# Wo read in 8 KB runs for pairs of heads, the two halves of each value product joined before the gather

## The chip, the cores and the metric

One core of a Trainium2 chip runs the kernel. The engines named here are PE (TensorE matmul, with its weight loads listed apart as PEld), DVE (VectorE), ACT (ScalarE), POOL (GpSimd) and SP (SyncE, which here only issues DMAs). The metric is the device time of one execution in microseconds. Before the change three runs gave 120.51, 120.59 and 120.69 us, with 120.59 us as their median.

## The reference, cut to what matters

```python
xn = layernorm(x)                              # x: 8 rows of 512
q  = (xn @ wq)                                 # 32 heads of 128
k, v = last 1024 positions of the caches       # 8 key-value heads, 4 query heads on each
p  = softmax(q k^T / sqrt(128))
s  = concat_heads(p v) @ wo                    # wo: 4096 x 512
h  = (gelu(xn @ w_gate) * (xn @ w_up)) @ w_down
out = x + s * silu(h)                          # 8 x 512
```

All tensors are bf16. The work is a decode step: the caches of eight sequences and the weights, 47 MB in all, are read once, and little is computed on each byte.

## The kernel before, in words

**Loads.** SP issues every large load in program order into nine rotating 2 MB buffers named big: wq, w_gate, w_up, then per key-value head one K tile and one V tile (2 MB each, in 8 KB runs per partition), w_down in between, and at the end wo. `load_wo` (L127) reads wo in five DMAs, listed in `pieces` (L623 to L625): four heads at once, two heads, one head, then three quarters and the last quarter of head 7. The 4096 rows of wo are laid out so that partition p of a head holds that head's rows 4p to 4p+3: a run of 4 KB.

**The loop.** A set s (16 of them, NS) is half of a key-value head's eight sequences: four sequences, 128 partitions. The loop at L571 runs half steps t, with s, i = divmod(t, 2). One half step writes to the engines' queues, in this order: the exponentials of set s-2 (ACT, L488), a transpose of a quarter of K (PE, L433) copied out by DVE (L444), on odd half steps from s = 6 the `gather` of a finished head (L580), another quarter of K copied out by ACT (L446), the transpose of the probabilities (DVE, L498), the scores of set s-1 (PE L455, then one DVE pass L463 that masks and takes the maximum), the maxima across partitions (PE L474, DVE L479), and half of a value product of the set (t - 9) / 2 (`value_half`, L504: eight PE matmuls, L509). The engines work through these queues in order; what an engine waits for holds back everything queued behind it.

**Values and gather.** The value product of a set lands in one PSUM bank, o_ps, as two halves of 128 columns, because V is read two positions to a partition row; only one half is meant for a given partition. ACT copies both halves to blk (L516, 128 x 256). A POOL copy (L492) puts the row sums beside the second half. `gather` (L520) multiplies, on PE, four times per head with a mask (sums) that picks the right half and adds up the partitions: 128 columns out, fp32. Then DVE takes the reciprocal of the row sum (L531), divides (L533), and turns the head's 128 x 128 block into oL (L541), which is the weight side of the output projection. The gather's result m_out and the maxima's result m_top lie in the same PSUM tile, m_ps.

**Projection.** After the loop, `project` (L609) runs four matmuls of 128 columns per query head (128 in all, L615) in the order of `pieces`, each piece waiting for its DMA; then two DVE operations (L633, L634) combine with g_sb and xf, and two small DMAs write the output.

Of the kernel before, what the change touches and what calls it, by code (L numbers as in the profile page):

```python
# [8 lines left out]
ACT = mybir.ActivationFunctionType  # L9
ALU = mybir.AluOpType  # L10
AX = mybir.AxisListType
BF16 = mybir.dt.bfloat16
FP32 = mybir.dt.float32
# [4 lines left out]
def kernel(  # L18
# [13 lines left out]
    nc = tc.nc  # L32

    B, Sq, D = A_x.shape
    Hkv, Sk, Dh = A_k_cache.shape[1], A_k_cache.shape[2], A_k_cache.shape[3]
    Hq = A_wq.shape[1] // Dh
    rep = Hq // Hkv
# [5 lines left out]
    scale = float(Dh) ** -0.5  # L43
    P = nc.NUM_PARTITIONS
# [6 lines left out]
    G = 4  # L51
    NB = B // G
# [4 lines left out]
    SET = NCH * Dh  # L57
# [3 lines left out]
    DP = Dh // 2  # L61
    NQB = D // 128
    PB = 32 // B

    NG = 2
    NS2 = NQB // NG
# [4 lines left out]
    big = ctx.enter_context(tc.tile_pool(name="big", bufs=9))  # L71
# [13 lines left out]


    m_ps = ps_m.tile([P, 512], FP32, name="m_ps")
    m_top, m_out = m_ps[:, 0:P], m_ps[:, P : P + Dh + 1]


    x_sb = rows.tile([B, D], BF16, name="x_sb")
# [23 lines left out]
                nc.sync.dma_start(out=t[:, y, :], in_=src[y])  # L115
        return [t[:, y, :].rearrange("p (c d) -> p c d", c=NCH) for y in range(NB)]

    HB = 2 * SET // (rep * D)
    wo_tiles = {}

    def wo_at(h):

        if h // HB not in wo_tiles:
            wo_tiles[h // HB] = big.tile([P, HB, rep * D], BF16, name="big")
        return wo_tiles[h // HB]

    def load_wo(h, r0, n, nh=1):  # L127

        t = wo_at(h)[:, h % HB : h % HB + nh, r0 * D : (r0 + n) * D]
        nc.sync.dma_start(  # L130
            out=t if nh > 1 else t[:, 0, :],
            in_=A_wo[h * rep * Dh : (h + nh) * rep * Dh, :].rearrange(
                "(h p r) n -> p h (r n)", p=P, r=rep
            )[:, :, r0 * D : (r0 + n) * D]
            if nh > 1
            else A_wo[h * rep * Dh : (h + 1) * rep * Dh, :].rearrange(
                "(p r) n -> p r n", r=rep
            )[:, r0 : r0 + n, :],
        )
        return [t[:, i, :].rearrange("p (r n) -> p r n", r=n) for i in range(nh)]  # L140

    wq_rows = []
    for k0, cuts in ((0, (1, 1)), (2, (2,))):
        t = big.tile([P, 2, Hq * Dh], BF16, name="big")
        i = 0
# [93 lines left out]
    quarter = consts.tile([P, NS2 + 32], FP32, name="quarter")  # L239
    nc.gpsimd.memset(quarter, 0.0)  # L240
    gsel = lead.tile([P, G], FP32, name="gsel")
    sums = consts.tile([P, 2, 2, rep, B, PB], FP32, name="sums")
    nc.gpsimd.memset(sums, 0.0)
    qT = qT0.rearrange("p (e s c g j) -> p e s c g j", e=2, c=2, g=G, j=rep)


    OW = 32
    OL = rep * OW
    oL = rows.tile([P, NS2 * (Hkv + 1), OL + 1], BF16, name="oL")
    nc.gpsimd.memset(oL, 0.0)  # L250

    def masks():
        nc.vector.tensor_reduce(
            out=parts, in_=identf.rearrange("p (x n) -> p n x", n=NC),
            axis=AX.X, op=ALU.max,
        )
        nc.vector.tensor_reduce(
            out=gsel, in_=parts.rearrange("p (g j) -> p g j", j=rep),
            axis=AX.X, op=ALU.max,
        )  # L260
        nc.vector.tensor_reduce(
            out=half, in_=identf.rearrange("p (r c n) -> p c r n", c=2, n=NC),
            axis=AX.XY, op=ALU.max,
        )
        nc.vector.tensor_reduce(
            out=quarter[:, NS2 : NS2 + B * NS2 : NS2],
            in_=identf.rearrange("p (a b f) -> p f b a", b=B, f=PB)[:, 0],
            axis=AX.X, op=ALU.max,
        )

        nc.vector.tensor_scalar(
            out=gsel, in0=gsel, scalar1=-1.0, scalar2=-NEG, op0=ALU.add, op1=ALU.mult
        )
        nc.vector.tensor_copy(
            out=own.rearrange("p c b g -> p (c b) g"),
            in_=gsel.unsqueeze(1).to_broadcast([P, CP * 32 // G, G]),
        )

        m = small.tile([P, NC], FP32, name="m16")
        nc.vector.tensor_scalar(  # L280
            out=m, in0=parts, scalar1=-1.0, scalar2=-NEG, op0=ALU.add, op1=ALU.mult
        )
        nc.vector.tensor_copy(
            out=same, in_=m.unsqueeze(1).to_broadcast([P, NR * 2, NC])
        )
        for c in range(2):
            for b in range(2):
                nc.vector.tensor_scalar(
                    out=sums[:, c, b].rearrange(
                        "p j (g y) f -> p y j g f", y=NB  # L290
                    )[:, b],
                    in0=parts.rearrange("p (g j) -> p j g", j=rep)
                    .unsqueeze(3).to_broadcast([P, rep, G, PB]),
                    scalar1=half[:, c : c + 1], scalar2=None, op0=ALU.mult,
                )

    hT = rows.tile([P, NFC, 32], BF16, name="hT")
# [7 lines left out]
    for k in range(NDC):  # L305
        w = wq_rows[k]
        for t in range(NT):
            for g in range(NQB):
# [3 lines left out]
                    w[:, 0, h * HD : (h + 1) * HD],  # L312
                    start=(k == 0), stop=(k == NDC - 1), skip_group_check=True,
                )
    q_row = rows.tile([P, NT, rep, 2, 2, DP], BF16, name="q_row")
    for c in range(2):
        nc.vector.tensor_copy(  # L317
            out=q_row[:, 0, :, :, c, :],
# [91 lines left out]

    def fold():

        f_sb = rows.tile([P, D], FP32, name="f_sb")
        nc.scalar.activation(out=f_sb, in_=f_state["ps"], func=ACT.Copy)
        spread(m_top, quarter, f_sb)
        f_state["ps"] = m_top[0 : 32 * NG]
# [66 lines left out]
        biases[s] = bias  # L483

    def exponentials(s):
        blk[s] = small.tile([P, 2, Dh + 1], FP32, name="blk", bufs=6)
        P_[s] = p_pool.tile([P, CP * 32], BF16, name="p")
        nc.scalar.activation(  # L488
            out=P_[s], in_=sc.pop(s), func=ACT.Exp, scale=scale, bias=biases.pop(s),
            accum_out=blk[s][:, 0, Dh : Dh + 1],  # L490
        )
        nc.gpsimd.tensor_copy(  # L492
            out=blk[s][:, 1, Dh : Dh + 1], in_=blk[s][:, 0, Dh : Dh + 1]
        )

    def turn(s):
# [2 lines left out]
            out=pT[s].rearrange("p c k -> p (c k)"), in_=P_.pop(s)  # L499
        )  # L500

    o_ps = {}

    def value_half(s, i):  # L504
        if i == 0:
            o_ps[s] = ps_o.tile([P, 2, Dh], FP32, name="o_ps")
        for c in range(i * CP // 2, (i + 1) * CP // 2):
            q = c % NR
            nc.tensor.matmul(  # L509
                o_ps[s][32 * q : 32 * q + 32].rearrange("p c d -> p (c d)"),  # L510
                pT[s][:, c, :],
                V[s][:, 2 * c : 2 * c + 2, :].rearrange("p c d -> p (c d)"),
                start=(c < NR), stop=(c >= CP - NR), skip_group_check=True,
            )
        if i == 1:
            nc.scalar.activation(out=blk[s][:, :, 0:Dh], in_=o_ps.pop(s), func=ACT.Copy)  # L516
            pT.pop(s)
            V.pop(s)

    def gather(h):  # L520

        ps = m_out
        for b in range(NB):
            t = blk.pop(h * NB + b)
            for c in range(2):
                nc.tensor.matmul(  # L526
                    ps, sums[:, c, b].rearrange("p j b f -> p (j b f)"), t[:, c, :],
                    start=(b == 0 and c == 0), stop=(b == NB - 1 and c == 1),
                )
        rec = small.tile([P, 1], FP32, name="rec")  # L530
        nc.vector.reciprocal(out=rec, in_=ps[:, Dh : Dh + 1])  # L531
        o = small.tile([P, rep, Dh // rep], BF16, name="o")
        nc.vector.tensor_scalar(  # L533
            out=o, in0=ps[:, 0:Dh].rearrange("p (i r) -> p r i", r=rep),
            scalar1=rec, scalar2=None, op0=ALU.mult,
        )


        out = oL[:, NS2 * h : NS2 * h + PB, 0:OL]
        out = out.rearrange("p f (r y) -> p r y f", y=OW)  # L540
        nc.vector.transpose(  # L541
            out=out[:, :, 0 : B * NS2 : NS2, :], in_=o.rearrange("p r i -> p (r i)")
        )


# [25 lines left out]
    for t in range(2 * NS + LV + 3):  # L571
# [3 lines left out]
        if s < NS:  # L575
            if i == 0 and s % NB == 0:
                fetch("K", s // NB)
            transpose_quarter(s, 2 * i)
        if i == 1 and s >= 6 and s % 2 == 0:
            gather((s - 6) // 2)  # L580
        if s < NS:
            transpose_quarter(s, 2 * i + 1)
        for _ in range(2):
# [5 lines left out]
            scores(s - 1)  # L589
        if i == 1 and 0 <= s - 1 < NS:  # L590
            maxima(s - 1)
        if t == LV - 1:
            fetch("D", 0)
            down(0)
# [11 lines left out]

    s_ps = ps_s.tile([32 * NG, 128], FP32, name="s")

    def project(h, r, w):  # L609
        t = oL[:, NS2 * h : NS2 * (h + 1)].rearrange("p f y -> p (f y)")  # L610
        for s in range(NS2):
            a = s * OL + r * OW
            for g in range(NG):
                q = NG * s + g
                nc.tensor.matmul(  # L615
                    s_ps[32 * g : 32 * g + 32, :], t[:, a : a + OW],
                    w[:, q * 128 : (q + 1) * 128],
                    start=(h == 0 and r == 0 and s == 0),
                    stop=(h == Hkv - 1 and r == rep - 1 and s == NS2 - 1),
                    skip_group_check=True,  # L620
                )

    pieces = [(0, 0, rep, 4), (4, 0, rep, 2), (6, 0, rep, 1)]  # L623

    pieces += [(Hkv - 1, 0, rep - 1, 1), (Hkv - 1, rep - 1, 1, 1)]  # L625
    for h0, r0, nr, nh in pieces:
        t = load_wo(h0, r0, nr, nh)
        for h in range(h0, h0 + nh):
            for r in range(r0, r0 + nr):
                project(h, r, t[h - h0][:, r - r0, :])  # L630
    tmp = small.tile([32 * NG, 128], FP32, name="tmp", bufs=1)
    out_sb = small.tile([32 * NG, 128], BF16, name="out_sb", bufs=1)
    nc.vector.tensor_tensor(out=tmp, in0=s_ps, in1=g_sb, op=ALU.mult)  # L633
# [36 lines left out]
```

## Time and profile before

| what | value |
|---|---|
| median of three runs | 120.59 us |
| time of the profiled execution | 120.65 us |
| span of the profiled execution | 118.8 us |
| bytes moved by DMA | 47.60 MB in 6569 packets |
| DMA queue q1 (SP's loads) | 95.2% of 16 engines over the span |
| PE / PEld busy | 84.4 us (71%) / 59.2 us (50%) |
| DVE / ACT / POOL busy | 66.3 (56%) / 56.2 (47%) / 7.5 us (6%) |

The span is the profiler's time from the first to the last instruction; the remaining 1.85 us of the execution lie around it. Busy times overlap between engines, so they do not add up to the span. An engine that is busy for 71% of the span may still have the last word in a stretch at the end, which is why stretches are looked at one by one.

### The profile page before, as it was taken

What the parts mean: (1) busy time and instruction counts of PE and PEld (TensorE: products, weight loads), DVE (VectorE), ACT (ScalarE), POOL (GpSimd) and SP (SyncE); (2) the same over time, 40 slices, a digit from 0 to 9 for tenths busy, and PEclk for the clock granted to TensorE, in tenths of its full rate; (3) what the DMA queues carried; (4) which work ended last, traced back from release to release, by engine and by line L of the source; (5) the groups of instructions that cost most, each with busy time, mean ns of one, the idle gap of its engine ahead of it and who ended that gap; (6) DMA issues with size and microseconds to landing.
All of it is one profiled execution on the core that took longest, in us unless ns stands there. A gap on an engine that the chain in (4) does not pass through costs nothing.

```text
span 118.8 us, 2387 instructions
## 1 busy us (share of the span) xinstructions
PE 84.4 (71%) x974; PEld 59.2 (50%) x974; DVE 66.3 (56%) x171; ACT 56.2 (47%) x94; POOL 7.5 (6%) x28
## 2 busy tenths in 40 slices
PE   0070629599492999699969869787795988676670
PEld 0020216198262677377746557555573755555660
DVE  1310131837799766678848658585773965834301
ACT  0500030229808667575854884676565577132000
POOL 7700000000000000000000000000000000000000
PEclk9999999999999599999999999999999999999997
DMA  3999999999999999999999999999999999999940
GB/s 94 430 450 436 406 444 405 433 430 419 422 462 412 412 428 433 417 428 428 425 425 428 422 436 422 422 433 425 425 425 425 428 428 430 408 421 421 420 170 3
DMA packets 6569, 47.60 MB, mean 401 GB/s; under 512 B 536, under 2 KB 672, under 8 KB 1696
## 3 DMA queue, kind: packets, MB, share of 16 engines
q1 hardware_dynamic: 6512, 47.45, 95.2%
q8 instruction: 7, 0.11, 0.3%
q10 hardware_dynamic: 48, 0.01, 0.1%
q14 instruction: 2, 0.02, 0.0%
HBM read 47.46 MB, written 0.01 MB: 400 GB/s over the span
## 4 chain that ended last, share of the span: by engine, by line
DMA 86%; SPq 6%; PE 4%; issue 0%; DVE 0%
DMA big<-in_A_k_cache_dram 72%; DMA big<-in_A_wo_dram 14%; SPq L130 4%; PE kT_ps L433 3%; SPq L147 1%; SPq L98 1%; PE s L615 1%; PE sc L455 0%; DVE tmp L633 0%; DVE out_sb L634 0%; PE o_ps L509 0%
## 5 line engine op out<-in xcount | busy, mean ns | idle before, releaser
L446 ACT ACTIVATE kT<-kT_ps 128x1024 bf16<-128x1024 bf16 x32 | 32.5, 1021 | 23.6 <-PE kT_ps L433 23.5
L433 PE MATMUL kT_ps<-identf,big 128*128 128x128 f32 x256 | 38.5, 296 | 5.2 <-DMA big<-in_A_k_cache_dram 5.1
L433 PEld LDWEIGHTS kT_ps<-identf,big 128*128 128x128 f32 x256 | 30.9, 151 | 13.2 <-DMA big<-in_A_k_cache_dram 7.0
L444 DVE COPY kT<-kT_ps 128x1024 bf16<-128x1024 bf16 x32 | 22.0, 688 | 15.2 <-PE kT_ps L433 15.0
L488 ACT ACTIVATE p<-sc_sb,bias 128x512 bf16<-128x512 f32 x16 | 11.5, 717 | 7.0 <-DVE bias L479 6.5
L509 PE MATMUL o_ps<-big,pT 128*32 128x256 bf16 x256 | 12.3, 274 | 3.0 <-ACT blk L516 1.6
L498 DVE STREAM_TRANSPOSE pT<-p 128x512 bf16<-128x512 bf16 x16 | 11.3, 704 | 2.8 <-ACT p L488 2.8
L474 PE MATMUL m_ps<-identf,top 128*128 128x128 f32 x32 | 7.3, 309 | 6.0 <-DVE top L463 4.3
L463 DVE CUSTOM_DVE_ANT_0 sc_sb<-sc,own 128x512 f32<-128x512 f32 x16 | 10.5, 656 | 0.5 <-PE sc L455 0.5
L455 PE MATMUL sc<-kT,zeros 128*32 128x512 bf16 x128 | 10.3, 398 | 0.5 <-ACT kT L446 0.5
L509 PEld LDWEIGHTS <-pT 128*32 128x32 bf16 x256 | 5.8, 94 | 8.0 <-DMA big<-in_A_v_cache_dram 2.2
L526 PE MATMUL m_ps<-blk,sums 128*128 128x129 f32 x64 | 9.3, 286 | 0.0
L492 POOL COPY blk<-blk 128x1 f32<-128x1 f32 x16 | 2.9, 184 | 96.5 <-ACT p L488 92.2
L474 PEld LDWEIGHTS m_ps<-identf,top 128*128 128x128 f32 x32 | 4.8, 187 | 8.1 <-DVE top L463 5.0
L526 PEld LDWEIGHTS m_ps<-blk,sums 128*128 128x128 f32 x64 | 8.1, 191 | 0.9 <-issue 0.2
L516 ACT ACTIVATE blk<-o_ps 128x256 f32<-128x256 f32 x16 | 6.1, 381 | 3.0 <-PE o_ps L509 3.0
L541 DVE STREAM_TRANSPOSE oL<-o 128x128 bf16<-128x128 bf16 x8 | 6.0, 748 | 0.3
L310 PE MATMUL sc<-big,zeros 128*32 128x512 bf16 x16 | 2.5, 611 | 4.6 <-DMA big<-in_A_wq_dram 4.2
L615 PE MATMUL s<-big,oL 128*32 128x128 bf16 x128 | 4.3, 219 | 1.9 <-DMA big<-in_A_wo_dram 1.9
L317 DVE CAST q_row<-sc 128x512 bf16<-128x512 f32 x2 | 1.3, 686 | 7.8 <-PE sc L310 7.8
L615 PEld LDWEIGHTS <-oL 128*32 128x32 bf16 x128 | 3.8, 96 | 2.5 <-issue 2.3
L479 DVE CUSTOM_DVE_ANT_0 scr<-m_ps,same 128x128 f32<-128x128 f32 x16 | 4.9, 304 | 0.1
(70 smaller groups left out, 51.5 us busy)
## 6 DMA issues: line engine op xcount, KB each, us to landing
big<-in_A_k_cache_dram SPq DMA_DIRECT2D x7, 2048.0 KB, 34.1
big<-in_A_v_cache_dram SPq DMA_DIRECT2D x7, 2048.0 KB, 33.1
big<-in_A_wq_dram SPq DMA_DIRECT2D x2, 1024.0 KB, 5.8
big<-in_A_wq_dram SPq DMA_DIRECT2D x1, 2048.0 KB, 11.2
big<-in_A_k_cache_dram SPq DMA_DIRECT2D x2, 1024.0 KB, 21.3
big<-in_A_v_cache_dram SPq DMA_DIRECT2D x2, 1024.0 KB, 30.3
big<-in_A_wo_dram SPq DMA_DIRECT2D x1, 2048.0 KB, 30.9
big<-in_B_w_gate_dram SPq DMA_DIRECT2D x1, 1792.0 KB, 15.0
```

Of the source, the lines that this page charges most:

```text
L433: nc.tensor.transpose(ps[:, c, :], K[s][:, 2 * (i * QP + c) : 2 * (i * QP + c) + 2, :] .rearrange("p c d -> p (c d)").bitcast(FP32), identf,)
L444: nc.vector.tensor_copy(out=out, in_=in_)
L446: nc.scalar.activation(out=out, in_=in_, func=ACT.Copy)
L455: nc.tensor.matmul(ps[32 * R : 32 * R + 32], qT[:, e, s].rearrange("p c b j -> p (c b j)"), t[:, :, 32 * R : 32 * R + 32, e], start=(e == ...
L463: nc.vector.tensor_tensor_reduce(out=sc[s], in0=ps.rearrange("p c k -> p (c k)"), in1=own.rearrange("p c b g -> p (c b g)"), op0=ALU.add, ...
L474: nc.tensor.matmul(ps, top.pop(s).to_broadcast([P, P]), identf, start=True, stop=True)
L488: nc.scalar.activation(out=P_[s], in_=sc.pop(s), func=ACT.Exp, scale=scale, bias=biases.pop(s), accum_out=blk[s][:, 0, Dh : Dh + 1],)
L498: nc.vector.transpose(out=pT[s].rearrange("p c k -> p (c k)"), in_=P_.pop(s))
L509: nc.tensor.matmul(o_ps[s][32 * q : 32 * q + 32].rearrange("p c d -> p (c d)"), pT[s][:, c, :], V[s][:, 2 * c : 2 * c + 2, :].rearrange("p ...
L516: nc.scalar.activation(out=blk[s][:, :, 0:Dh], in_=o_ps.pop(s), func=ACT.Copy)
L526: nc.tensor.matmul(ps, sums[:, c, b].rearrange("p j b f -> p (j b f)"), t[:, c, :], start=(b == 0 and c == 0), stop=(b == NB - 1 and c == 1),)
L615: nc.tensor.matmul(s_ps[32 * g : 32 * g + 32, :], t[:, a : a + OW], w[:, q * 128 : (q + 1) * 128], start=(h == 0 and r == 0 and s == 0), s ...
```

## The change

Wo is read for pairs of heads: partition p of a pair holds the pair's rows 8p to 8p+7, a run of 8 KB. The pieces become two pairs, one pair, and the last pair in runs of 4, 3 and 1 rows (4 KB, 3 KB, 1 KB). Because a pair's rows are dealt out to the partitions by eights, the weight side oL must hold both heads of a pair turned together.

The two halves of a value product are joined before the gather: ACT copies the first half with a per-partition factor of 0 or 1 (128 x 128 in place of 128 x 256), and a new DVE operation, `join`, multiplies the second half (read from PSUM) by the other factor and adds it. The POOL copy of the row sums goes. `join` stands in the next half step, behind the DVE copy of a K quarter. Since o_ps is now read by ACT and then by DVE, the value products use two PSUM banks in turn.

`gather` still has four fp32 matmuls per head, each now with 64 columns of weights, and writes the 64 partitions of m_out that belong to the head of the pair. It moves one half step later (to i = 0, s odd). The division and the turn leave `gather`; a new function `finish` does them once per pair, in the half step after the second head's gather: one reciprocal of two columns, two multiplications of 128 x 64, one turn of 128 x 256. f_sb takes over the memory of q_row.

```diff
-    m_top, m_out = m_ps[:, 0:P], m_ps[:, P : P + Dh + 1]
+    m_top = m_ps[:, 0:P]
+    m_out = m_ps[:, P : P + 2 * (Dh + 1)].rearrange("p (a d) -> p a d", a=2)
...
-    HB = 2 * SET // (rep * D)
+    R8 = 2 * rep
+    HB = 2 * SET // (R8 * D)
     wo_tiles = {}
-    def wo_at(h):
-        if h // HB not in wo_tiles:
-            wo_tiles[h // HB] = big.tile([P, HB, rep * D], BF16, name="big")
-        return wo_tiles[h // HB]
-    def load_wo(h, r0, n, nh=1):
-        t = wo_at(h)[:, h % HB : h % HB + nh, r0 * D : (r0 + n) * D]
-        nc.sync.dma_start(
-            out=t if nh > 1 else t[:, 0, :],
-            in_=A_wo[h * rep * Dh : (h + nh) * rep * Dh, :].rearrange(
-                "(h p r) n -> p h (r n)", p=P, r=rep
-            )[:, :, r0 * D : (r0 + n) * D]
-            if nh > 1
-            else A_wo[h * rep * Dh : (h + 1) * rep * Dh, :].rearrange(
-                "(p r) n -> p r n", r=rep
-            )[:, r0 : r0 + n, :],
-        )
-        return [t[:, i, :].rearrange("p (r n) -> p r n", r=n) for i in range(nh)]
+    def wo_at(m):
+        if m // HB not in wo_tiles:
+            wo_tiles[m // HB] = big.tile([P, HB, R8 * D], BF16, name="big")
+        return wo_tiles[m // HB]
+    def load_wo(m, r0, n, nm=1):
+        t = wo_at(m)[:, m % HB : m % HB + nm, r0 * D : (r0 + n) * D]
+        src = A_wo.rearrange("(m p k) n -> p m (k n)", p=P, k=R8)
+        src = src[:, m : m + nm, r0 * D : (r0 + n) * D]
+        if nm == 1:
+            nc.sync.dma_start(out=t[:, 0, :], in_=src[:, 0, :])
+        else:
+            nc.sync.dma_start(out=t, in_=src)
+        return [t[:, i, :].rearrange("p (r n) -> p r n", r=n) for i in range(nm)]
...
-    sums = consts.tile([P, 2, 2, rep, B, PB], FP32, name="sums")
+    sums = consts.tile([P, NB, 2, rep // 2, B, PB], FP32, name="sums")
...
-    OL = rep * OW
-    oL = rows.tile([P, NS2 * (Hkv + 1), OL + 1], BF16, name="oL")
+    OL = R8 * OW
+    oL = rows.tile([P, NS2 * (Hkv // 2 + 1), OL + 1], BF16, name="oL")
...
-        for c in range(2):
-            for b in range(2):
-                nc.vector.tensor_scalar(
-                    out=sums[:, c, b].rearrange(
-                        "p j (g y) f -> p y j g f", y=NB
-                    )[:, b],
-                    in0=parts.rearrange("p (g j) -> p j g", j=rep)
-                    .unsqueeze(3).to_broadcast([P, rep, G, PB]),
-                    scalar1=half[:, c : c + 1], scalar2=None, op0=ALU.mult,
+        for b in range(NB):
+            for a in range(2):
+                nc.vector.tensor_copy(
+                    out=sums[:, b, a].rearrange("p j (g y) f -> p y j g f", y=NB)[:, b],
+                    in_=parts.rearrange("p (g j a) -> p a j g", a=2, g=G)[:, a]
+                    .unsqueeze(3).to_broadcast([P, rep // 2, G, PB]),
...
-        f_sb = rows.tile([P, D], FP32, name="f_sb")
+        f_sb = rows.tile([P, 2 * NT * HD], BF16, name="q_row")[:, 0 : 2 * D].bitcast(FP32)
...
-        blk[s] = small.tile([P, 2, Dh + 1], FP32, name="blk", bufs=6)
+        blk[s] = small.tile([P, Dh + 1], FP32, name="blk", bufs=7)
         P_[s] = p_pool.tile([P, CP * 32], BF16, name="p")
         nc.scalar.activation(
             out=P_[s], in_=sc.pop(s), func=ACT.Exp, scale=scale, bias=biases.pop(s),
-            accum_out=blk[s][:, 0, Dh : Dh + 1],
-        )
-        nc.gpsimd.tensor_copy(
-            out=blk[s][:, 1, Dh : Dh + 1], in_=blk[s][:, 0, Dh : Dh + 1]
+            accum_out=blk[s][:, Dh : Dh + 1],
...
-    o_ps = {}
+    o_ps, joins = {}, []
+    def join():
+        s = joins.pop()
+        o = blk[s][:, 0:Dh]
+        nc.vector.scalar_tensor_tensor(
+            out=o, in0=o_ps.pop(s)[:, 1, :], scalar=half[:, 1:2], in1=o,
+            op0=ALU.mult, op1=ALU.add,
+        )
     def value_half(s, i):
         if i == 0:
-            o_ps[s] = ps_o.tile([P, 2, Dh], FP32, name="o_ps")
+            if s % 2 == 0 and s > 0:
+                o_ps[s] = ps_s.tile([P, 2, Dh], FP32, name="s")
+            else:
+                o_ps[s] = ps_o.tile([P, 2, Dh], FP32, name="o_ps")
...
-            nc.scalar.activation(out=blk[s][:, :, 0:Dh], in_=o_ps.pop(s), func=ACT.Copy)
+            nc.scalar.activation(
+                out=blk[s][:, 0:Dh], in_=o_ps[s][:, 0, :], func=ACT.Copy,
+                scale=half[:, 0:1],
+            )
+            joins.append(s)
...
-        ps = m_out
-        for b in range(NB):
-            t = blk.pop(h * NB + b)
-            for c in range(2):
+        x = h % 2
+        t = [blk.pop(h * NB + b) for b in range(NB)]
+        for a in range(2):
+            for b in range(NB):
                 nc.tensor.matmul(
-                    ps, sums[:, c, b].rearrange("p j b f -> p (j b f)"), t[:, c, :],
-                    start=(b == 0 and c == 0), stop=(b == NB - 1 and c == 1),
-                )
-        rec = small.tile([P, 1], FP32, name="rec")
-        nc.vector.reciprocal(out=rec, in_=ps[:, Dh : Dh + 1])
-        o = small.tile([P, rep, Dh // rep], BF16, name="o")
-        nc.vector.tensor_scalar(
-            out=o, in0=ps[:, 0:Dh].rearrange("p (i r) -> p r i", r=rep),
-            scalar1=rec, scalar2=None, op0=ALU.mult,
-        )
-        out = oL[:, NS2 * h : NS2 * h + PB, 0:OL]
+                    m_out[64 * x : 64 * x + 64, a, :],
+                    sums[:, b, a].rearrange("p j b f -> p (j b f)"), t[b],
+                    start=(b == 0), stop=(b == NB - 1), skip_group_check=True,
+                )
+    def finish(h):
+        rec = small.tile([P, 2], FP32, name="rec")
+        nc.vector.reciprocal(out=rec, in_=m_out[:, :, Dh])
+        o = small.tile([P, R8, 2, Dh // R8], BF16, name="o", bufs=2)
+        for a in range(2):
+            nc.vector.tensor_scalar(
+                out=o[:, :, a, :],
+                in0=m_out[:, a, 0:Dh].rearrange("p (i r) -> p r i", r=R8),
+                scalar1=rec[:, a : a + 1], scalar2=None, op0=ALU.mult,
+            )
+        m = h // 2
+        out = oL[:, NS2 * m : NS2 * m + PB, 0:OL]
         out = out.rearrange("p f (r y) -> p r y f", y=OW)
         nc.vector.transpose(
-            out=out[:, :, 0 : B * NS2 : NS2, :], in_=o.rearrange("p r i -> p (r i)")
+            out=out[:, :, 0 : B * NS2 : NS2, :], in_=o.rearrange("p r a d -> p (r a d)")
...
-        if i == 1 and s >= 6 and s % 2 == 0:
-            gather((s - 6) // 2)
+        if joins:
+            join()
+        if i == 0 and s >= 7 and s % 2 == 1:
+            gather((s - 7) // 2)
...
+        if i == 1 and s >= 9 and s % 4 == 1:
+            finish((s - 7) // 2)
...
-    def project(h, r, w):
-        t = oL[:, NS2 * h : NS2 * (h + 1)].rearrange("p f y -> p (f y)")
+    def project(m, r, w):
+        t = oL[:, NS2 * m : NS2 * (m + 1)].rearrange("p f y -> p (f y)")
...
-    pieces = [(0, 0, rep, 4), (4, 0, rep, 2), (6, 0, rep, 1)]
-    pieces += [(Hkv - 1, 0, rep - 1, 1), (Hkv - 1, rep - 1, 1, 1)]
-    for h0, r0, nr, nh in pieces:
-        t = load_wo(h0, r0, nr, nh)
-        for h in range(h0, h0 + nh):
+    last = Hkv // 2 - 1
+    pieces = [(0, 0, R8, 2), (2, 0, R8, 1)]
+    pieces += [(last, 0, rep, 1), (last, rep, rep - 1, 1), (last, R8 - 1, 1, 1)]
+    for m0, r0, nr, nm in pieces:
+        t = load_wo(m0, r0, nr, nm)
+        for m in range(m0, m0 + nm):
             for r in range(r0, r0 + nr):
-                project(h, r, t[h - h0][:, r - r0, :])
+                project(m, r, t[m - m0][:, r - r0, :])
```

More of the change, by code (lines that the diff above doesn't have):

```diff
@@ L314 @@
                 )
-    q_row = rows.tile([P, NT, rep, 2, 2, DP], BF16, name="q_row")
+    q_row = rows.tile([P, 2 * NT * HD], BF16, name="q_row").rearrange(
+        "p (t j e c w) -> p t j e c w", t=NT, j=rep, e=2, c=2
+    )
     for c in range(2):
@@ L617, in project @@
                     w[:, q * 128 : (q + 1) * 128],
[L618 to L619 removed]
+                    start=(m == 0 and r == 0 and s == 0),
+                    stop=(m == Hkv // 2 - 1 and r == R8 - 1 and s == NS2 - 1),
                     skip_group_check=True,
                 )
[L623 to L628 removed]
+    last = Hkv // 2 - 1
[4 more added lines that the diff above has]
+        for m in range(m0, m0 + nm):
             for r in range(r0, r0 + nr):
[L630 removed]
+                project(m, r, t[m - m0][:, r - r0, :])
     tmp = small.tile([32 * NG, 128], FP32, name="tmp", bufs=1)
```

## The prediction

> **What bounds the kernel now.** I read the profile page first, then the chain that ended last, then a table of stretches, then the timeline of the last 30 us. From the page:
>
> ```profile
> DMA  3999999999999999999999999999999999999940
> DMA packets 6569, 47.60 MB, mean 401 GB/s; under 512 B 536, under 2 KB 672, under 8 KB 1696
> q1 hardware_dynamic: 6512, 47.45, 95.2%
> DMA 86%; SPq 6%; PE 4%; issue 0%; DVE 0%
> ```
>
> The DMA row is at 9 in every slice but the first and the last two, and the chain is 86% DMA: from about 1.5 us to 115 us the 16 engines are never short of work, so the time is the bytes' time plus a head and a tail. What changes the time is the rate at which bytes move, or a tail that ends after the last byte. The table of stretches (us, busy time and instructions per engine, granted PE clock, DMA share, GB/s) prices the first:
>
> ```profile
> 90.00:100.00 10.00, 8.11 (x96) 5.94 (x100) 6.68 (x17) 6.26 (x12) 0.37 (x2) 1.00 1.01 427
> 105.50:111.50 6.00, 4.58 (x89) 3.88 (x90) 2.54 (x6) 1.09 (x3) 0.00 (x0) 1.00 1.03 422
> 112.00:115.00 3.00, 2.03 (x61) 1.61 (x55) 0.00 (x0) 0.00 (x0) 0.00 (x0) 1.00 0.73 284
> ```
>
> From 90 to 100 us only 8 KB packets of K and V move, at 427 GB/s; from 105.5 to 111.5 only the 4 KB packets of wo, at 422. After 112 the engines run dry one by one (share 0.73). The timeline of the tail prices the second:
>
> ```profile
> 93.06 1.06 PE L526 MATMUL m_ps<-blk,sums 128*128 128x129 f32 x8
> ...
> 95.64 0.40 PE L509 MATMUL o_ps<-big,pT 128*32 128x256 bf16 x8 [0.39 <-DMA big<-in_A_v_cache_dram]
> ...
> 102.65 0.49 PE L474 MATMUL m_ps<-identf,top 128*128 128x128 f32 x2 [0.65 <-DVE o L533]
> ...
> 104.76 0.62 PE L509 MATMUL o_ps<-big,pT 128*32 128x256 bf16 x16 [1.08 <-ACT blk L516]
> ...
> 108.17 1.27 PE L526 MATMUL m_ps<-blk,sums 128*128 128x129 f32 x8
> ...
> 110.06 0.75 DVE L541 STREAM_TRANSPOSE oL<-o 128x128 bf16<-128x128 bf16 x1
> 110.37 1.96 PE L615 MATMUL s<-big,oL 128*32 128x128 bf16 x64 [0.94 <-DMA big<-in_A_wo_dram]
> 112.82 1.07 PE L615 MATMUL s<-big,oL 128*32 128x128 bf16 x32 [0.48 <-DMA big<-in_A_wo_dram]
> 114.11 0.62 PE L615 MATMUL s<-big,oL 128*32 128x128 bf16 x16 [0.22 <-DMA big<-in_A_wo_dram]
> 115.05 0.62 PE L615 MATMUL s<-big,oL 128*32 128x128 bf16 x16 [0.31 <-DMA big<-in_A_wo_dram]
> ```
>
> Every group of projection matmuls waited for a DMA. A projection matmul takes 1.96/64 = 0.031 us; the 112 ahead of the last 16 take 3.43 us. PE was through with the last gather at 109.44 and so could have begun the last 16 at 112.87; they began at 115.05. The compute tail has 2.2 us of cover.
>
> **The change part by part.**
>
> *Wo in 8 KB runs.* Three of the four MB change from 768 packets of 4 KB to 384 of 8 KB; the last MB keeps its 4, 3 and 1 KB runs (512, 384, 128 KB, as in the DMA list of before), and there are five DMAs before and after. 3.146 MB at 422 GB/s is 7.45 us, at 427 it is 7.37: a gain of 0.09 us. The trace's single packet records give another value: 309 ns for 8192 bytes and 159 for 4096, so 24 pairs on each engine save 24 x 9 = 0.22 us; but successive packets of an engine overlap by 3 to 4 ns each, and from start to start it is 306 against 155.5 twice, 24 x 5 = 0.12 us. I take **0.12 us**, between the ends 0 and 0.35; the upper end adds to the 0.22 the stretch from 102 to 106 us, where V's end and wo's start moved at 413 GB/s: 4 us x 14/427 = 0.13 us, if all of that were the 4 KB packets' doing.
>
> By the Trainium skill, DMA: Bandwidth & Descriptors, section Specifications, line rate needs packets of only 512 B, so 4 KB packets would lose nothing and the gain would be nil. The 422 against 427 GB/s do not bear that out fully.
>
> *Less on ACT and POOL.* L516 shrinks from 128x256 (381 ns) towards L421's 64x128 (271 ns); I take 0.28, 16 x 0.10 = 1.6 us of ACT. The 16 POOL copies of 184 ns go; POOL idles 96 us around them. Worth nothing in time while DMA binds.
>
> *`join` on DVE.* The nearest row is L479, a 128x128 pass over PSUM and SBUF: 304 ns. I take 0.30 (ends 0.2 and 0.4): 16 x 0.30 = 4.8 us more DVE. It is queued behind the K-quarter copy and ahead of the maxima's DVE pass, on which the exponentials wait. In the steady loop PE waits 1.05, 1.12 and 1.24 us for each of the last three K tiles (at 71.0, 80.8, 90.8 us) and 0.4 us per V tile, so up to 1.1 us per head is covered and no load is held back: SP issues loads 15 to 34 us ahead of landing. If that cover were gone, loads would still be queued for tens of us.
>
> *`finish` in place of the division.* Before, 8 x (0.168 + 0.351 + 0.748) = 10.1 us of DVE. After, 4 x (0.17 + 2 x 0.26 + turn): a 128x64 multiply is half-way between L533's 0.351 and a small pass of 0.17. The turn of 128x256 I price from L541, 0.748 us for 128 strided columns, against L498, 0.704 us for 512 dense ones: the dense rate leaves some 0.17 us fixed, so 4.5 ns per strided column, and 256 of them take 1.33 (ends 0.75 and 1.5). One finish is 2.0 us on DVE in one piece.
>
> *The start.* The masks' four passes (248 ns) become four smaller ones, oL's memset grows from 2.03 to about 2.25 us, that of sums halves (0.515). All is done long before the first K tile lands at 23.8 us: nothing. f_sb in q_row's memory waits for transposes that ended some 15 us earlier: nothing.
>
> *The gather moved and the tail.* This can cost. PE start-to-start costs from the timeline around 90 us: a K quarter 0.52, scores 0.44, a value half 0.31, maxima 0.34, a gather 0.89. I add up the new order from the landing of V5 (95.62 us):
> 1. Before, the gather at 93.06 stood in the shadow of the wait for V5. Now it comes after it, between two K quarters, and shifts all behind it by 0.89: the last scores begin at 100.85, not 99.96.
> 2. At 102.65 maxima waited behind gather and division. Without these, and with one join on DVE, maxima begin at 102.9 and the last exponentials at 103.75 (before 103.63). The 0.9 us is nearly won back.
> 3. Gather 5 now runs beside the exponentials; with two banks the waits on ACT (1.08 us at 104.76) go, and the second half of set 13 ends at 105.6 (before 105.38).
> 4. `finish` of heads 4 and 5 takes DVE from 105.55 to 107.6. The join of set 13 queues behind it until 107.9, gather 6 on PE waits for that join, and the second half of set 14 and all of set 15 are queued behind gather 6. Gather 6 is issued by 108.8 (ended before: 106.58).
> 5. Three value halves to 109.75, ACT's copy to 110.08, join to 110.42, gather 7 to **111.3**. The same adding-up done for the old order ends 0.4 us later than measured, so 110.9 to 111.3, against 109.44: 1.5 to 1.9 us of the cover of 2.2 is used.
> 6. Then 112 matmuls, 3.43 us: PE is ready for the last 16 at 114.3 to 114.75; their data, 0.12 us earlier than before, at 114.93. The last `finish` is off the path: 111.5 + 0.2 + 0.52 + 1.33 = 113.5, wanted once 96 matmuls are through at 113.9 or later.
>
> What remains is 0.2 to 0.6 us of cover; with the ends of the turn and the join, from nil to 1.2.
>
> **Sum.** The profiled execution took 120.65 us: span 118.8 plus 1.85 around it. It becomes 120.65 - 0.12 = 120.53. It stood 0.06 above the median of the runs, so the median becomes 120.59 - 0.12 = **120.47 us**. That is 0.1% and lies inside 0.2% (0.24 us), about what a measurement of this kernel can tell from no change.
>
> **The rivals.**
> - *The tail overruns.* From the point where gather 7 ends after 114.93 - 3.43 = 111.5 us, each further us adds one. Against it: my sum ends 0.2 to 0.6 us short of that point. For it: step 4 is a chain of four queues in order, each of which adds its semaphore, and a turn slower than 1.5 us or a join that collides with ACT on the same bank would each count in full. With gather 7 at 112.3 us PE would be ready at 115.73, 0.8 us late: 120.47 + 0.8 = 121.27 us. To be slower by over 0.24 us against 120.59 it must end after 111.86.
> - *The packets are worth more.* If the lower rate from 102 to 106 us (413 GB/s) is the 4 KB packets' doing and not that of an instruction fetch (part of queue q8's seven packets, each holding one DMA engine), the gain is up to 0.35: about 120.27 us. For it: the packet durations' 0.22. Against it: 413 is a mix of V and wo.
> - *The packets are worth nothing*, because the last DMA engine to finish is late for other reasons (share 0.73 at the end): 120.59 us.
>
> **How the numbers follow.** Tail fits and 0.12 is won, 0.35, time 120.47. Nothing won, 0.08, 120.59. More won, 0.27, about 120.27. Tail overruns enough to show, 0.30, from 120.85 up, middle 121.2. So faster 0.27, same 0.43, slower 0.30. The likeliest case alone spans 120.36 to 120.6. The range for 8 in 10 goes from 120.2, near the far end of the packets' gain, to 121.4, which leaves out the worst third of the overruns.
>
> **What would show it.** Right: 8 KB packets near 427 GB/s between 105 and 110 us, 768 fewer packets under 8 KB, all last matmul groups still waiting on wo's DMA, the last gather at 110.9 to 111.3 us, the join near 0.30 and the turn near 1.33 us. Wrong: the last projection matmuls released by a gather or by oL and not by a DMA; a DMA row with gaps before 112 us; a chain that ends on DVE and PE lines instead of DMA.

## The result, and the profile after

The change made the kernel slower and unsteady. Nineteen runs of it gave a median of 121.93 us, from 120.62 to 123.47; nineteen runs of the kernel before gave 120.69 us, from 120.51 to 120.83. The ratio of the two is 1.0052, 95% interval 1.0026 to 1.0077; it leaves out runs more than 1.5% above the fastest of their kernel, here seven of the nineteen, but such times come back with this order of compute in two of the experiments below, and in none of the 69 runs of the kernel before, so the medians, 1% apart, belong beside it. The forecast was 120.47 us with a range up to 121.4: the time lies above the range.

The profiled execution took 121.9 us, its span is 119.8 us. From its page, the granted clock in 40 slices, the packets, and the chain that ended last:

```profile
PEclk9999999958998699999999999999999999997699
DMA packets 6186, 47.60 MB, mean 397 GB/s; under 512 B 537, under 2 KB 673, under 8 KB 929
DMA 76%; PE 11%; DVE 4%; SPq 3%; ACT 2%; issue 1%
DMA big<-in_A_v_cache_dram 53%; DMA big<-in_A_k_cache_dram 22%; PE m_ps L538 4%; PE s L637 3%; PE kT_ps L431 2%; SPq L145 1%; PE s L516 1%; DVE oL L559 1%; SPq L116 1%; SPq L99 1%; PE o_ps L516 1%; DVE blk L502 1%; ACT p L486 1%; ACT kT L444 1%; ACT blk L524 1%
```

The packets under 8 KB fell from 1696 to 929: wo is read as intended. But in the chain wo is gone. Before, the last link of DMA was wo itself; now the chain leaves the loads with V and runs to the end through the gather (L538), the projection (L637), the turn (L559), the join (L502) and ACT's copy (L524). The tail of the timeline, in order:

```profile
105.94 0.35 DVE L502 SCALAR_TENSOR_TENSOR blk<-s,half,blk 128x128 f32<-128x128 f32 x1 [0.28 <-ACT blk L524]
...
107.05 1.31 DVE L559 STREAM_TRANSPOSE oL<-o 128x256 bf16<-128x256 bf16 x1
...
108.00 0.48 DVE L502 SCALAR_TENSOR_TENSOR blk<-o_ps,half,blk 128x128 f32<-128x128 f32 x1
...
108.53 0.87 PE L538 MATMUL m_ps<-blk,sums 128*64 128x129 f32 x6 [1.03 <-DVE blk L502]
...
109.57 1.08 PE L516 MATMUL o_ps<-big,pT 128*32 128x256 bf16 x16
...
111.50 1.55 PE L538 MATMUL m_ps<-blk,sums 128*64 128x129 f32 x6 [0.17 <-DVE blk L502]
...
112.98 3.75 PE L637 MATMUL s<-big,oL 128*32 128x128 bf16 x128
...
113.94 1.34 DVE L559 STREAM_TRANSPOSE oL<-o 128x256 bf16<-128x256 bf16 x1
116.78 0.28 DVE L656 TENSOR_TENSOR tmp<-s,g_sb 64x128 f32<-64x128 f32 x1 [1.49 <-PE s L637]
```

The turn at 107.05 holds the join of set 13 at 108.00, which holds gather 6 (the gather of head 6), which holds the value products behind it. All 128 projection matmuls run in one block with no wait for a DMA: each piece of wo had landed before PE came to it. And six gather matmuls of the same shape take 0.87 us at 108.53 and 1.55 us at 111.50. The stretches show why (us, busy time and instructions of PE, PEld, DVE, ACT, POOL, then granted PE clock, DMA share, GB/s):

```profile
106.19:109.60 3.41, 1.90 (x28) 1.19 (x31) 2.22 (x6) 0.15 (x1) 0.00 (x0) 0.99 1.03 435
109.60:113.02 3.42, 3.25 (x34) 1.94 (x24) 0.70 (x2) 0.73 (x2) 0.00 (x0) 0.51 0.99 408
113.02:116.43 3.41, 3.41 (x125) 3.41 (x126) 2.12 (x4) 0.00 (x0) 0.00 (x0) 1.00 0.29 109
```

From 109.60 to 113.02 us PE was granted half its clock. In the 3.41 us before, it had been busy for 1.90 us, waiting for joins in between.

Of the signs that the prediction had named, two of those for being wrong came: the projection's last matmuls were not released by a DMA, and the chain ends on PE and DVE lines. The sign of the packets came as well. From 105 to 110 us, where wo now moves in 8 KB packets, the rate rose from 421 to 426 GB/s (before, then after):

```profile
105.00:110.00 5.00, 3.95 (x64) 3.05 (x53) 1.95 (x6) 1.16 (x3) 0.00 (x0) 1.00 1.02 421
105.00:110.00 5.00, 3.23 (x59) 2.13 (x60) 3.12 (x7) 0.89 (x3) 0.00 (x0) 0.96 1.01 426
```

### The profile page after: what moved, and what is told of

The parts are those of the page before. It is cut to its first block, busy times and chain, and to the rows that moved or that the text cites. A ratio compares the mean times of both kernels' runs of the same rounds, so it can differ in the third digit from the quotient of the medians.

```text
span 119.8 us, 2373 instructions
## 1 busy us (share of the span) xinstructions
PE 84.3 (70%) x974; PEld 57.8 (48%) x974; DVE 69.1 (58%) x179; ACT 55.7 (46%) x94; POOL 4.6 (4%) x12
## 4 chain that ended last, share of the span: by engine, by line
DMA 76%; PE 11%; DVE 4%; SPq 3%; ACT 2%; issue 1%
DMA big<-in_A_v_cache_dram 53%; DMA big<-in_A_k_cache_dram 22%; PE m_ps L538 4%; PE s L637 3%; PE kT_ps L431 2%; SPq L145 1%; PE s L516 1%; DVE oL L559 1%; SPq L116 1%; SPq L99 1%; PE o_ps L516 1%; DVE blk L502 1%; ACT p L486 1%; ACT kT L444 1%; ACT blk L524 1%
## 5 line engine op out<-in xcount | busy, mean ns | idle before, releaser
L431 PE MATMUL kT_ps<-identf,big 128*128 128x128 f32 x256 | 38.0, 292 | 2.8 <-DMA big<-in_A_k_cache_dram 2.8
L431 PEld LDWEIGHTS kT_ps<-identf,big 128*128 128x128 f32 x256 | 29.5, 148 | 11.6 <-PE sc L453 2.5
L516 PEld LDWEIGHTS <-pT 128*32 128x32 bf16 x256 | 6.4, 97 | 10.6 <-issue 6.4
L538 PE MATMUL m_ps<-blk,sums 128*64 128x129 f32 x64 | 10.1, 300 | 1.6 <-DVE blk L502 1.2
L538 PEld LDWEIGHTS m_ps<-blk,sums 128*64 128x64 f32 x64 | 7.4, 146 | 4.1 <-DVE blk L502 2.3
L516 PE MATMUL s<-big,pT 128*32 128x256 bf16 x112 | 5.6, 276 | 5.1 <-DMA big<-in_A_v_cache_dram 4.5
L516 PE MATMUL o_ps<-big,pT 128*32 128x256 bf16 x144 | 7.5, 290 | 0.7 <-DVE blk L502 0.4
L559 DVE STREAM_TRANSPOSE oL<-o 128x256 bf16<-128x256 bf16 x4 | 5.3, 1336 | 0.2
L318 ACT ACTIVATE q_row<-o_ps 128x512 bf16<-128x512 f32 x2 | 1.1, 594 | 7.8 <-PE o_ps L305 7.8
L524 ACT ACTIVATE blk<-s,half 128x128 f32<-128x128 f32 x7 | 2.5, 364 | 4.1 <-PE s L516 4.1
```

Source lines behind the costliest of these rows:

```text
L431: nc.tensor.transpose(ps[:, c, :], K[s][:, 2 * (i * QP + c) : 2 * (i * QP + c) + 2, :] .rearrange("p c d -> p (c d)").bitcast(FP32), identf,)
L516: nc.tensor.matmul(o_ps[s][32 * q : 32 * q + 32].rearrange("p c d -> p (c d)"), pT[s][:, c, :], V[s][:, 2 * c : 2 * c + 2, :].rearrange("p ...
L538: nc.tensor.matmul(m_out[64 * x : 64 * x + 64, a, :], sums[:, b, a].rearrange("p j b f -> p (j b f)"), t[b], start=(b == 0), stop=(b == NB ...
L559: nc.vector.transpose(out=out[:, :, 0 : B * NS2 : NS2, :], in_=o.rearrange("p r a d -> p (r a d)"))
```

## The experiments

Two theories stood after the result. The tail theory: `finish` and the joins in DVE's queue make the last gather late, and PE can no longer finish the projection by the time wo has landed. The clock theory adds that PE's waits in the tail halve its clock in the next stretch, which would explain the spread. The rivals: the 8 KB reads themselves, the join's time throughout the loop, or the order on PE alone.

### The packets alone

The kernel before, with the DMAs of the changed one:

```diff
-    pieces = [(0, 0, rep, 4), (4, 0, rep, 2), (6, 0, rep, 1)]
-    pieces += [(Hkv - 1, 0, rep - 1, 1), (Hkv - 1, rep - 1, 1, 1)]
+    pieces = [(0, 0, R8, 2), (2, 0, R8, 1)]
+    pieces += [(last, 0, rep, 1), (last, rep, rep - 1, 1), (last, R8 - 1, 1, 1)]
...
-                project(h, r, t[h - h0][:, r - r0, :])
+                project(2 * m + r // rep, r % rep, t[m - m0][:, r - r0, :])
```

> The kernel before with only wo's DMAs changed to 8 KB runs of head pairs; the weight side still has the old row order, so the projection multiplies the wrong rows of wo (same operations and sizes). Tail theory (the loss of the change comes from its compute tail, the packets gain a little): 0.1 us faster than before, 120.5 to 120.6 us, with the small spread of before. Rival, the 8 KB reads themselves disturb the end of the DMA stream: 121 us or more, or a spread of over 1 us. By the packet durations alone (309 against 2 x 159 ns) 0.22 us faster.

Measured: 120.57 us (120.44 to 120.78, 11 runs) against 120.65; ratio 0.999, interval 0.9982 to 0.9999. The packets are worth some 0.1%, by the interval at most 0.2%, and disturb nothing. In its profile a half-clock stretch happened to fall into the tail as well:

```profile
102.37:105.78 3.41, 1.94 (x37) 1.41 (x38) 1.94 (x5) 1.31 (x4) 0.18 (x1) 0.99 1.02 430
105.78:109.19 3.41, 2.92 (x36) 2.19 (x38) 1.26 (x3) 0.54 (x2) 0.00 (x0) 0.51 1.01 428
```

and still the last matmuls waited for wo, from the timeline:

```profile
109.46 1.27 PE L523 MATMUL m_ps<-blk,sums 128*128 128x129 f32 x8
...
112.83 1.07 PE L612 MATMUL s<-big,oL 128*32 128x128 bf16 x32 [0.20 <-DMA big<-in_A_wo_dram]
...
115.07 0.62 PE L612 MATMUL s<-big,oL 128*32 128x128 bf16 x16 [0.31 <-DMA big<-in_A_wo_dram]
```

That execution took 120.56 us. Its last gather ended at 110.73 us, 1.3 us later than in the profile before (109.44), and the time did not move. The old order can have the same clock dips; it has the cover to swallow them.

### The order alone

The changed kernel with wo in 4 KB runs again:

```diff
-    pieces = [(0, 0, R8, 2), (2, 0, R8, 1)]
-    pieces += [(last, 0, rep, 1), (last, rep, rep - 1, 1), (last, R8 - 1, 1, 1)]
+    pieces = [(0, 0, rep, 4), (4, 0, rep, 2), (6, 0, rep, 1)]
+    pieces += [(Hkv - 1, 0, rep - 1, 1), (Hkv - 1, rep - 1, 1, 1)]
...
-                project(m, r, t[m - m0][:, r - r0, :])
+                project(h // 2, rep * (h % 2) + r, t[h - h0][:, r - r0, :])
```

> The changed kernel with only wo's DMAs put back to the old 4 KB runs per head (wrong rows again in the projection, same operations). Tail theory: as the changed kernel, a median near 121.9 us and a spread of 2 us or more between runs, since the queues are the same and the end is set by PE and not by the last byte. Rival, the packets do it: 120.6 to 120.8 us with the spread of before.

Measured: 121.84 us (120.65 to 123.59, 12 runs), the changed kernel's time and spread; ratio 1.0035, interval 1.0011 to 1.0058, worked out as above. From its timeline, the last gather and the projection:

```profile
112.15 1.13 PE L542 MATMUL m_ps<-blk,sums 128*64 128x129 f32 x6 [0.16 <-DVE blk L506]
113.21 3.75 PE L641 MATMUL s<-big,oL 128*32 128x128 bf16 x128
```

Again one block of 128 without a wait for wo. The loss lies in the order of the compute; the packets have no part in it that these runs can show.

### The turn one step later

```diff
+        turned[h] = o
+    def turn_pair(h):
+        o = turned.pop(h)
...
             finish((s - 7) // 2)
+        if i == 1 and s >= 10 and s % 4 == 2:
+            turn_pair((s - 8) // 2)
```

> The changed kernel with one edit: the turn of a pair (1.34 us of DVE) is queued one step later than its division, behind the next join. Tail theory: the join of set 13 no longer waits for the turn, gather 6 and all behind it come 1.2 us earlier, PE is ready for the last 16 matmuls before their data, and the time falls to 120.5 to 120.8 us, with less spread. Rival, the join itself or the moved gather costs the time: no gain, 121.5 us or more.

Measured: 120.78 us (120.53 to 121.0, 11 runs); ratio to the kernel before 1.0007, interval 0.9998 to 1.0016. From its timeline:

```profile
106.96 0.34 DVE L502 SCALAR_TENSOR_TENSOR blk<-o_ps,half,blk 128x128 f32<-128x128 f32 x1
...
107.22 1.30 DVE L563 STREAM_TRANSPOSE oL<-o 128x256 bf16<-128x256 bf16 x1
...
109.42 1.31 PE L538 MATMUL m_ps<-blk,sums 128*64 128x129 f32 x8 [0.42 <-DVE blk L502]
...
114.93 0.62 PE L644 MATMUL s<-big,oL 128*32 128x128 bf16 x16 [0.31 <-DMA big<-in_A_wo_dram]
```

The join now stands ahead of the turn, at 106.96 instead of 108.00; the last gather ends at 110.73 instead of 113.05, and the last group waits for wo again. This profile's tail ran at full clock, so not all of the 2.3 us is the turn's; the next experiment gives the changed kernel's tail at full clock, 111.83. In the eleven runs nearly all of the loss and the spread are gone: to put this one kind of DVE operation elsewhere in its queue is enough. The joins themselves stayed, so their time in the loop is not what cost the 1%. The edit moved three turns, that of the tail and two in the loop, and doesn't tell their shares apart.

### Matmuls that keep PE busy

```diff
+    def filler(n):
+        ps = ps_kT.tile([P, 512], FP32, name="kT_ps")
+        for _ in range(n):
+            nc.tensor.matmul(ps, ident, zeros[:, 0:512], start=True, stop=True)
...
+        if t == 33:
+            filler(4)
...
+        if t == 37:
+            filler(7)
```

> The changed kernel with matmuls that compute nothing used, put on PE where it idles in the tail: four ahead of the last maxima, seven behind the first half of set 14 (about 0.22 us each at full clock, fitting into waits of 1.2 and 1.8 us). Clock theory (PE's idle stretches in the tail halve the granted clock in the following 3.4 us, where the last gather and the projection lie): the clock stays at 1.00 from 106 us to the end, the time falls to 120.7 to 121.1 us and the spread shrinks below 1 us. Tail theory without the clock: no gain, since the added matmuls can only delay; 121.9 us or more.

Measured: median 120.78 us; ten of twelve runs from 120.71 to 120.98, two at 122.03 and 122.28; ratio 1.0026, interval 1.0001 to 1.0051. Stretches and timeline of its profile:

```profile
104.55:107.97 3.42, 2.84 (x43) 1.64 (x42) 2.74 (x7) 1.02 (x4) 0.00 (x0) 1.00 1.02 431
107.97:111.38 3.41, 2.98 (x40) 1.98 (x39) 1.13 (x4) 0.74 (x2) 0.00 (x0) 1.00 1.00 420
```

```profile
106.83 1.46 PE L591 MATMUL kT_ps<-zeros,ident 128*128 128x512 bf16 x6 [0.16 <-issue]
...
108.22 1.11 PE L538 MATMUL m_ps<-blk,sums 128*64 128x129 f32 x8
...
110.52 1.31 PE L538 MATMUL m_ps<-blk,sums 128*64 128x129 f32 x8 [0.42 <-DVE blk L502]
111.76 3.81 PE L646 MATMUL s<-big,oL 128*32 128x128 bf16 x128
```

More work on PE made the kernel faster by 1.1 us in the median. The added matmuls feed nobody, and the clock stayed at 1.00 through the tail: this speaks for the clock theory. They moved nothing else that mattered: gather 6 ended at 109.33 us, without them at 109.40. From there to the end of the last gather it took 2.50 us here and 3.65 us in the first profile, so half clock cost 1.15 us. The two runs above 122 us have no profile; what slowed them is open. The profile also shows the tail at full clock: the last gather ends at 111.83, the projection is still one block, and it ends at 115.57 us, just where the old kernel's DMA-bound projection ended (115.67). At full clock the change comes out nearly even; at half clock it loses.

### Both the turn and gather 6 later

```diff
-        if i == 0 and s >= 7 and s % 2 == 1:
+        if i == 0 and s >= 7 and s % 2 == 1 and s != 19:
...
             value_half(s3, i3)
+        if t == 40:
+            gather(6)
...
+        if i == 1 and s in (10, 14, 20):
+            turn_pair(1 if s == 10 else 3 if s == 14 else 5)
```

> The changed kernel with the turn behind its next joins (for heads 4 and 5 behind the last join) and gather 6 queued on PE behind the whole value product of set 15, just ahead of gather 7. Tail theory: with neither the turn nor gather 6 in the way, the last gather ends near 109.7 us, as early as before the change, PE has 1.5 us or more of cover, the packets' 0.1 us is kept: 120.5 to 120.6 us with the small spread of before, and all last projection matmuls wait for wo's DMA even where a half-clock window falls into the tail. Rival, something else in the new order costs 0.1 us: 120.7 us or more, as with the turn alone put later.

Measured: 120.69 us (120.57 to 120.82, 11 runs) against 120.68; ratio 1.0002, interval 0.9993 to 1.0011. The spread is that of the kernel before, even though half clock struck in the tail of the profiled execution:

```profile
100.57:103.99 3.42, 1.65 (x26) 0.77 (x25) 2.04 (x8) 1.55 (x4) 0.00 (x0) 0.99 1.01 419
103.99:107.40 3.41, 3.38 (x32) 2.49 (x33) 1.10 (x3) 1.18 (x3) 0.00 (x0) 0.51 1.01 428
```

```profile
95.06 0.49 PE L472 MATMUL m_ps<-identf,top 128*128 128x128 f32 x2
...
108.94 1.80 PE L538 MATMUL m_ps<-blk,sums 128*64 128x129 f32 x16
...
114.89 0.62 PE L646 MATMUL s<-big,oL 128*32 128x128 bf16 x16 [0.31 <-DMA big<-in_A_wo_dram]
```

The last gather ended at 110.74 us, later than the 109.7 that I expected; the half-clock stretch lies ahead of it, and no profile shows it at full clock. The kernel doesn't beat the one before: wo's last data released the matmuls at 114.89 instead of 115.05, but the 0.1% of the packets does not show in the time. Where that went is open; with the interval's lower end at 0.9993 it may be there in part.

### Gather 6 alone later

The two edits to the gather above, on the changed kernel, with the turn left in its place.

> The changed kernel with gather 6 alone queued later on PE; the turn of heads 4 and 5 still stands ahead of the join of set 13 on DVE. Tail theory: the set-15 value product still needs the bank that the join of set 13 frees (108.4 us), but not gather 6 as well, so the last gather ends about 0.5 us earlier than in the changed kernel: 120.6 to 121.5 us with a spread of about 1 us, between the changed kernel and the one with the turn put later. Rival, the order on PE is what matters and not the DVE block: as good as with the turn put later, 120.8 us.

Measured: 121.66 us (121.02 to 122.44, 4 runs), ratio 1.0104, interval 1.0059 to 1.0149; above what I expected. From its timeline:

```profile
93.43 1.36 DVE L559 STREAM_TRANSPOSE oL<-o 128x256 bf16<-128x256 bf16 x1
...
96.55 0.49 PE L472 MATMUL m_ps<-identf,top 128*128 128x128 f32 x2 [1.27 <-DVE top L461]
...
104.51 0.49 PE L472 MATMUL m_ps<-identf,top 128*128 128x128 f32 x2 [1.19 <-DVE top L461]
...
109.32 0.48 DVE L502 SCALAR_TENSOR_TENSOR blk<-o_ps,half,blk 128x128 f32<-128x128 f32 x1
109.85 0.62 PE L516 MATMUL o_ps<-big,pT 128*32 128x256 bf16 x16 [1.56 <-DVE blk L502]
...
110.41 1.80 PE L538 MATMUL m_ps<-blk,sums 128*64 128x129 f32 x16
```

Set 15's value product still waits 1.56 us for the bank that the join behind the turn frees. Even so the tail itself became shorter: from the last maxima (104.51) to the end of the last gather (112.21) it took 7.70 us at full clock, against 8.73 us with the fillers (103.10 to 111.83) and 7.52 with the turn late (103.21 to 110.73). So the order on PE does count, and the four runs (two near 121.05 us, two at 122.26 and 122.44) do not show it as worthless; what this profile lost, it lost ahead of the tail. The first two lines show that second effect, which I had not thought of. In this profile and in the one before, a half-clock stretch began near 87 us. With the turn put later the maxima of set 13 came at 95.06, ahead of V5's landing at 95.6, and nothing was lost; with the turn in its place they came at 96.55, past it, because the turn of heads 2 and 3 held up DVE's copies of K, and the tail started 1.4 us late.

### The changed kernel, run twice more

> The changed kernel once more, for another profile. Clock theory: the half-clock windows stand at another place; if one falls between 106 us and the end, the time is 121.5 us or more, and if none does, 120.6 to 120.9 us with the last 128 projection matmuls in one unbroken run of about 3.8 us. Rival, the spread has nothing to do with the clock: no such tie.

> The same as the run before it, once more: a half-clock window in the tail goes with 121.5 us or more, none with 120.6 to 120.9 us.

The first took 122.06 us, with half clock from 108.32 to 111.73 us. The second took 123.65 us, with two such stretches. Each is shown behind the stretch ahead of it, the first run's, then the second's:

```profile
104.91:108.32 3.41, 1.79 (x36) 0.95 (x34) 3.06 (x7) 0.73 (x2) 0.00 (x0) 0.99 1.01 428
108.32:111.73 3.41, 3.25 (x32) 2.21 (x32) 0.45 (x2) 0.61 (x2) 0.00 (x0) 0.51 1.01 424
```

```profile
93.05:96.46 3.41, 1.82 (x19) 1.21 (x17) 2.71 (x8) 1.75 (x3) 0.00 (x0) 0.99 1.02 432
96.46:99.88 3.42, 3.42 (x18) 2.43 (x20) 1.31 (x2) 0.29 (x3) 0.00 (x0) 0.51 1.00 424
106.70:110.12 3.42, 1.65 (x36) 0.93 (x35) 2.99 (x7) 0.73 (x2) 0.00 (x0) 0.99 1.00 424
110.12:113.53 3.41, 3.41 (x32) 2.19 (x32) 0.38 (x2) 0.73 (x2) 0.00 (x0) 0.51 0.97 396
```

From the second run's timeline:

```profile
110.10 1.55 PE L538 MATMUL m_ps<-blk,sums 128*64 128x129 f32 x6 [1.03 <-DVE blk L502]
...
114.71 3.75 PE L637 MATMUL s<-big,oL 128*32 128x128 bf16 x128
```

The projection began at 114.71 us, against 112.98 in the first profile and 111.76 with the fillers. One half-clock stretch from 96 us to the end of the compute went with 121.9 and 122.06 us (and with 121.98 in the profile with wo in 4 KB runs), two with 123.65. The nineteen runs fall into three heaps (six from 120.62 to 120.90, six from 121.49 to 122.26, seven from 123.04 to 123.47), which none, one and two such stretches would explain. The lowest heap of this kernel was not caught in a profile, so for it that is an inference from the kernel with the fillers.

## Why the prediction was wrong, point by point

**The bound.** That the loads set the end as long as the tail keeps its cover was right; every kernel whose profile shows the last group waiting for wo had a median of 120.57 to 120.78 us.

**Wo in 8 KB runs.** 0.12 us forecast; 0.1% measured alone, from 0.01 to 0.22 us by the interval. The start-to-start interval of the packets (0.12) and the rates (0.09) both fit; the packet durations' 0.22 lies at the interval's end. By the rule of the Trainium skill, DMA: Bandwidth & Descriptors, section Specifications, the gain would have been nil. The measurement's interval just excludes that. But in the profile with the packets alone the last data released PE at 115.07 us, against 115.05 before, and the kernel with both parts later shows no gain either, so the gain is not firmly shown.

**ACT's copy.** 0.28 us forecast, 0.364 to 0.37 measured. The saving that I counted is nearly absent (0.381 before), and ACT's copy stands in the tail's chain. The row that I had priced it from (L421) has half the partitions and no per-partition factor; which of the two makes the difference no run here shows.

**Join, multiplications, turn.** The turn was priced at 1.33 us and took 1.31 to 1.35; with 0.748 us for half the columns that is 4.4 to 4.7 ns per strided column, about as I had reckoned. The join took 0.35, not 0.30, and 0.48 behind a turn. The two multiplications took 0.61 together, not 0.52.

**The gather moved and the tail: the step that failed.** The mechanism of steps 1 to 5 is in the trace link by link. Its times fell short little by little: maxima at 103.18 (forecast 102.9), the last exponentials at 104.10 (103.75), set 13 ended at 105.92 (105.6), `finish` began at 106.21 (105.55) and ended at 108.36 (107.6), gather 6 ended at 109.40 (108.8). Each is 0.3 to 0.8 us late. Part of that is the terms above. Step 4 also lacks a term: the join of set 12 stands ahead of `finish` in DVE's queue, waited for ACT's copy, ran from 105.94 and held `finish` until 106.21. The rest is the hand-over from engine to engine, for which I had allowed too little, and for which I even took 0.4 us off, since my adding-up had come out late on the old order. At full clock, with the fillers, gather 7 ended at 111.83 where I had 110.9 to 111.3: that alone passes my tipping point of 111.5 and uses up the cover.

Step 5 then failed outright. It allowed 2.5 us from the end of gather 6 to that of gather 7, which is what the fillers' profile took (2.50); but it priced this at full clock, and in the first profile the clock was at half for nearly all of it: it took 3.65 us, until 113.05. Of the 1.75 us by which gather 7 came after 111.3, 0.6 had come about by gather 6 and 1.15 is the clock. Step 6, the projection, was priced about right; it began too late. I had read clock rows of 1.00 in the tail of one profile as a property of the tail. The same profile showed 0.72 between 36 and 42 us, and I didn't ask what makes it fall. So the cover that decided the forecast, 0.2 to 0.6 us, wasn't there at either clock.

**The loop's cover.** I said that up to 1.1 us per head is covered. It is, at full clock. Gather 6 alone later, and the second of the two further runs, show the delay from a half-clock stretch that began before 100 us arriving in the tail.

**The rivals.** The one that came true was the overrun, with a chance of 0.30; its mechanism (the queues of step 4) was right, its price (middle 121.2, against 121.93 measured) too low, because it held no clock. The range's upper end came from it. The fault was to treat 0.2 to 0.6 us of cover, the difference of two sums of some 16 us, as more likely to hold than not.

## What to carry to other kernels

A kernel bound by its loads has a hidden second deadline: what compute must still do after the last operand lands. When an edit uses that cover, look at DVE's queue for long operations that nobody needs soon standing ahead of short ones that PE waits for; moving the 1.3 us turns behind the 0.35 us joins brought back almost all of the 1% lost here. And price a tail at half the PE clock too, before calling it covered.

## What the runs showed of the hardware

The granted PE clock dropped to half for stretches of 3.41 us; in each of the two further runs, two followed each other directly once (from 46.9 and from 31.6 us). Apart from the second of such a pair, those that I looked at came behind an equally long stretch in which PE had been busy at part only: 0.86 us of 3.41 ahead of the dip in the middle of the kernel before (38.67 us), and between 1.65 and 1.94 us ahead of those shown above. The Trainium skill, TensorE: Matmul & The Clock Gate, section Part 1: The HAM clock gate, has the clock halve after at least one idle window of some 3.4 us on a grid that does not start with the kernel. The width and the shifting place agree with these traces; but the stretches ahead were half busy, not idle. A low busy share did not always bring a dip: in the profile with gather 6 alone later PE was busy for 1.74 us from 107.55 to 110.97 us, and no dip came, so the exact condition stays open. The dip in the kernel before with the stretch ahead of it, then that stretch and the one behind it:

```profile
35.26:38.67 3.41, 0.86 (x8) 0.68 (x7) 3.13 (x9) 2.64 (x4) 0.18 (x1) 0.99 1.02 436
38.67:42.08 3.41, 3.41 (x21) 2.24 (x20) 2.24 (x7) 1.84 (x3) 0.18 (x1) 0.51 0.99 415
```

```profile
107.55:110.97 3.42, 1.74 (x38) 1.32 (x39) 2.48 (x8) 0.85 (x3) 0.00 (x0) 1.00 1.00 422
110.97:114.38 3.41, 3.41 (x94) 3.16 (x93) 2.37 (x5) 0.00 (x0) 0.00 (x0) 1.00 0.85 340
```

That would also explain why one program has three times: the dips stand at another place in each profile (109.60, 108.32, and 96.46 with 110.12 us for the changed kernel), and the place decides what they delay. It is an inference from three profiles. In the old order (a dip at 105.78), and in the one with the turn and gather 6 later (at 103.99), dips in the tail cost nothing that shows, because loads cover them.
